# When thirteen stores of zeros are issued: a two-layer decode kernel, forward and backward, on one Trainium2 core

## The chip, the core and the metric

The kernel runs on one core of one Trainium2 chip. A core has a matrix engine (TensorE, PE in the profile; PEld is its weight load), a vector engine (VectorE, DVE), a scalar engine (ScalarE, ACT), a general engine (GpSimd, POOL) and SyncE (SP), which here only issues DMA transfers. All transfers run on 16 DMA engines. SyncE, ScalarE and GpSimd can each issue them: those of SyncE and ScalarE appear in the profile as "hardware_dynamic", those of GpSimd as "software_dynamic". The metric is the time of one launch in device microseconds. Four runs of the kernel before gave 444.23 to 446.92 us, median 445.85.

## What is computed

The reference is the gradient of four residual layers on a single token of width 1024: attention A, MLP B, attention A, MLP B, with the same weights both times. It returns the output, and the gradients of the input, of both caches and of all weights.

```python
def A(x, k_cache, v_cache, wq, wo):      # 32 heads of 128, 4 groups
    W = 4096                             # of 32768 positions, the last ones
    q = x @ wq                           # 1024 x 4096
    p = softmax(q @ k[last W].T * 128**-0.5)
    return (p @ v[last W]) @ wo          # 4096 x 1024
def B(x, w1, b1, w2):                    # 1024 x 3584, 3584 x 1024
    h = x @ w1 + b1
    return (h * tanh(softplus(h))) @ w2
x = x + A(layernorm(x)); x = x + B(layernorm(x))
x = x + A(layernorm(x)); x = x + B(layernorm(x))
out, vjp = jax.vjp(...)                  # returns (out, *vjp(grad_out))
```

Attention looks only at the last 4096 of 32768 cache positions. The gradient of both caches is therefore zero on the other 28672 positions, and these zeros have to be written: 58.7 MB, over half of what the kernel writes (98.84 MB). They depend on nothing, so the kernel may write them at any time.

## The kernel before

Everything is bf16 in memory. The order of the instructions on each engine is the order of the program text; each engine works through its own list, and waits only for what an instruction reads, writes or needs as a buffer. The stages, in order, with their place in the profiled execution (us):

- A1 forward, from 0: K, wq, V and part of wo are loaded and stay.
- B2 forward, from about 59: w1 streams in as 16 half-rows, w2 as 14 chunks of 512 KB through six buffers (`strm`, tag "st"), which all later streams share.
- A3 forward, from about 107.
- B4, 140 to 184 (`mlp_turn`, L711): forward and backward in one. It runs over seven blocks `b` of 512 columns of w1. A block loads two halves (L708), forms h in PSUM, takes mish and its derivative on ACT and DVE (`mish_exp` at L570 first writes y = min(h, 20), L576, then its exponential; `mish_y` at L587 later overwrites y), writes dh and a, and multiplies the transposed block by dh. Between blocks, PE transposes kept weights (`fill`).
- A3 backward, to about 236 (`attn_bwd`, L814).
- The second pass over w2 (`W2Pass.rest`, L646), to about 266: for each of 14 chunks c, PE multiplies and transposes, and DVE forms a row product with a reduction, which yields column c of `wg`.
- The w1 backward (`mlp_bwd_w1`, L795, with `w1_T`, L785), to about 294: 16 steps over half-rows of w1. T(i) loads half-row i and transposes it with PE; ACT and DVE copy the result back over the tile; M(i) multiplies it by dh. The order is M(0), T(2), M(1), T(3) and so on; T(0) and T(1) are put into the end of the w2 pass (hooks "w1", "w1b"). Six buffers hold the tiles, so the load of half-row i can start when M(i - 6) is done.
- A1 backward, to about 329.
- The dW stage, to the end: a list of jobs (L1052, L1285 to L1291) makes the weight gradients of w2, w1, dV, wo, dK, wq as outer products. PE writes PSUM, ACT and DVE evacuate it into 32 buffers, SyncE stores them. `weave` mixes the jobs of two gradients; a few preparing steps (`late_prep`) are inserted at fixed places of the list.

The zeros are cut into 112 stores of 512 KB (L122 to L126), all from one zeroed tile `zt`. Two helpers issue them. `zeros(n)` (L128) lets SyncE issue n of them at its place in SyncE's list. `bg_zeros(n, after)` (L134) lets GpSimd issue n: first a copy of one column of the tile `after`, whose only purpose is that GpSimd waits until that tile is written (a gate), then the stores. Nothing waits for a store of zeros but the end of the kernel, and GpSimd or SyncE themselves, when too many of their transfers are outstanding.

How many are issued where stands in the table `Z` (L1155): `B4` for the seven blocks; `B4w` for chunks of the second w2 pass; `W1` for the start of the w1 backward, behind dh; `W1m`, the steps i at which one store is issued, its gate being the tile of step i - 1; `A1c` in the A1 backward, on GpSimd; `A1d`, later there, on SyncE, where 100 means all that are left. In the kernel before, GpSimd issues 82 stores and SyncE 30.

Of the kernel before, what the change touches and what calls it, by code (L numbers as in the profile page):

```python
# [23 lines left out]
def kernel(  # L24
# [40 lines left out]
    NW2 = TF // 2  # L65
# [11 lines left out]
    def pair_col(kind, lname, n):  # L77

        if kind not in pairs:
            pairs[kind] = keep.tile([P, 2, n], BF16, name=f"{kind}_pair")  # L80
        return pairs[kind][:, 0 if lname in ("A3", "B4") else 1, :]
# [46 lines left out]
    def zeros(n):  # L128
        for _ in range(min(n, len(zero_jobs))):
            nc.sync.dma_start(zero_jobs.pop(0), zt[:])  # L130
# [3 lines left out]
    def bg_zeros(n, after):  # L134

        if n:
            nc.gpsimd.tensor_copy(gate_t[:], after[:, 0:1])
        for _ in range(min(n, len(zero_jobs))):
            nc.gpsimd.dma_start(zero_jobs.pop(0), zt[:])  # L139
# [47 lines left out]
    def xpose(blocks, dst, how=None, six=False):  # L187

        n = len(blocks)
        pools["turn"] += 1  # L190
        if six and pools["turn"] % 6 > 3:
            ps = shaped(pools["top"].tile([P, 1024], BF16, name="tps", tag="h"), [P, 8, P])
        else:
            ps = psum1([P, 8, P], BF16, "tps")
        for b, ap in enumerate(blocks):
            nc.tensor.transpose(ps[:, b, :], ap, ident_bf[:])  # L196
        evac(dst, ps[:, 0:n, :].rearrange("p b c -> p (b c)"), 0.08 * n + 0.05, 0.11 * n + 0.15, how)
# [21 lines left out]
    def wide(n):  # L219
        return Wide(pacc.tile([P, 512], FP32, name="acc", tag="acc"), n)  # L220

    def mv(acc, k, lhsT, vec, start, stop):
        mm(acc.col(k), lhsT, vec.to_broadcast([P, R16]), start, stop)
# [49 lines left out]
    def fill(n, keys, how=None, six=False):  # L273
        for i in range(n):
            for k in keys:
                if xq[k]:
                    ap = xq[k].pop(0)
                    xpose(*nat_blocks(ap), None if how is None else how[i % len(how)], six)
                    break

    def level():
        ev[:] = [0.0, 0.0]

    def ln_fwd(x_col, name):
        xx = work.tile([P, 2 * TD], FP32, name="xx")
        nc.vector.tensor_copy(xx[:, 0:TD], x_col[:])
        nc.vector.tensor_mul(xx[:, TD:], x_col[:], x_col[:])
        sps = sm_tile(P, 2 * TD)
        nc.tensor.matmul(sps[:], lhsT=onesD, rhs=xx[:], start=True, stop=True)
        if name == "A3":  # L290
            warm(6)
        s12 = work.tile([P, 2], FP32, name="s12")
        nc.vector.reduce_sum(s12[:], sps[:].rearrange("p (a b) -> p a b", a=2), axis=AX.X)
        var = work.tile([P, 1], FP32, name="var")
        nc.vector.scalar_tensor_tensor(out=var[:], in0=s12[:, 0:1], scalar=s12[:, 0:1], in1=s12[:, 1:2],
                                       op0=ALU.mult, op1=ALU.subtract, reverse1=True)
        lnv = work.tile([P, 1], FP32, name="lnv")
        nc.scalar.activation(lnv[:], var[:], ACT.Ln, bias=eps_t[:, 0:1], scale=1.0)
        rstd = keep.tile([P, 1], FP32, name=f"rstd_{name}")
        nc.scalar.activation(rstd[:], lnv[:], ACT.Exp, scale=-0.5)  # L300
        n_bf = pair_col("n" + name[0], name, TD)
        nc.vector.tensor_scalar(out=n_bf, in0=x_col[:], scalar1=s12[:, 0:1], scalar2=rstd[:, 0:1], op0=ALU.subtract, op1=ALU.mult)
        n32 = keep.tile([P, TD], FP32, name=f"n32_{name}")
        nc.vector.tensor_scalar(out=n32[:], in0=x_col[:], scalar1=s12[:, 0:1], scalar2=rstd[:, 0:1], op0=ALU.subtract, op1=ALU.mult)
        return n32, n_bf, rstd
# [44 lines left out]
    def wo_load(c):  # L350
        if c < NR:
            w = wo_kept[c]
        else:
            w = strm.tile([P, 2, D], BF16, name="wo_c", tag="st")[:]
        nc.sync.dma_start(w, wo_v[c])
        return w
# [83 lines left out]
    def attn_fwd(x_col, lname, first):  # L440
# [30 lines left out]
        if not first:  # L471
            for c in range(NR, min(NO, NR + NB)):
                held[c] = wo_load(c)
            bg_zeros(Z["A3"], n_bf)
            for w in wq_t:
# [94 lines left out]
    def mish_exp(h_ps, n):  # L570

        def wt(nm):
            return work.tile([P, HQ], FP32, name=nm, tag=nm)[:, 0:n]

        m = {k: wt(k) for k in ("u", "s_", "w_", "r", "hr", "y")}
        nc.vector.tensor_scalar(out=m["y"], in0=h_ps, scalar1=20.0, scalar2=None, op0=ALU.min)  # L576
        nc.scalar.activation(m["u"], m["y"], ACT.Exp)
        return m
# [90 lines left out]
    def mlp_fwd(x_col, lname, g_bf):  # L669
# [5 lines left out]
        for i in range(2 * TD):  # L675
            t, hf = i // 2, i % 2
            w = w1_load(i)
            if i == 0:
                bg_zeros(Z["B2a"], x_col)
            if i == 4:  # L680
# [17 lines left out]
        sv["dact"] = dact  # L698
        x_new, wg = w2.rest(0, g_bf, x_col, f"x_{lname}", gbc, Z["B2"], last)
        return x_new, sv, wg  # L700
# [10 lines left out]
    def mlp_turn(x_col, lname, wg, g_col, nxt):  # L711

        n32, n_bf, rstd = ln_fwd(x_col, lname)
        fill(6, ["V"], "av")
        level()
        sv = dict(n32=n32, rstd=rstd)
        a_bf = pair_col("a", lname, TF)
        dh = keep.tile([P, TF], FP32, name=f"dh_{lname}")
        dh_bf = pair_col("dh", lname, TF)
        sv["dh"], sv["dh_bf"], sv["a_bf"] = dh, dh_bf, a_bf  # L720
        wgf = wg[:].rearrange("p c t -> p (c t)")
        nacc = wide(TD)
        ws = {}
        FB = CB // P

        def M(b):
            w, lo = ws.pop(b), b * FB
            for t in range(TD):
                for f in range(FB):
                    o = (t % HT) * CB + f * P  # L730
                    mv(nacc, t, w[t // HT][:].rearrange("p t f -> p (t f)")[:, o:o + P], dh_bf[:, lo + f:lo + f + 1],
                       b == 0 and t == 0 and f == 0, b == NBK - 1 and f == FB - 1)

        def lo0(b):
            return max(b - 1, 0) * FB

        def X(b, hh):
            wf = ws[b][hh][:].rearrange("p t f -> p (t f)")
            for k in range(2):
                xpose(*alt_blocks(wf[:, k * 1024:(k + 1) * 1024], 4), None, True)  # L740

        for b in range(NBK):
            bg_zeros(Z["B4"][b], dh_bf[:, lo0(b):] if b else n_bf)
            ws[b] = [w1_block(b, hh) for hh in range(2)]
            lo = b * FB
            sl = slice(lo, lo + FB)
            hps = Wide(pacc.tile([P, FB * R16], FP32, name="sm", tag="sm"), FB)
            h_init(hps.t, lo, FB)
            for t in range(TD):
                for f in range(FB):  # L750
                    o = (f // 2) * 2 * P + f % 2
                    mv(hps, f, ws[b][t // HT][:, t % HT, o:o + 2 * P - 1:2], n_bf[:, t:t + 1], False, t == TD - 1)
            m = mish_exp(hps.cols(0, FB), FB)
            X(b, 0)
            mish_w(m, hps.cols(0, FB))
            q = work.tile([P, HQ], FP32, name="q_", tag="hr2")[:, 0:FB]
            nc.vector.tensor_mul(q, wgf[:, sl], m["r"])
            mish_y(m)
            nc.vector.tensor_mul(dh_bf[:, sl], m["y"], q)
            nc.vector.tensor_mul(dh[:, sl], m["y"], q)  # L760
            nc.vector.tensor_mul(a_bf[:, sl], m["hr"], m["w_"])
            ev[0] += 2.4
            ev[1] += 0.3
            if b:
                M(b - 1)
            X(b, 1)
            fill(4, ["wo", "V", "K", "wq"], None, True)
        M(NBK - 1)
        fill(2, ["wo", "V", "K", "wq"], "a")
        g_new, g_bf = ln_bwd(nacc.cols(0, TD), n32, rstd, g_col, lname, nxt)  # L770
        fill(100, ["wo"], "av")
        fill(4, ["V", "K", "wq"], "av")
        level()
        return g_new, g_bf, sv
# [10 lines left out]
    def w1_T():  # L785
# [3 lines left out]
        ws[i] = w  # L789
        if i in Z["W1m"]:  # L790
            bg_zeros(1, ws[i - 1])
# [3 lines left out]
    def mlp_bwd_w1(g_col, lname, sv, nxt):  # L795
# [13 lines left out]
        level()  # L809
        bg_zeros(Z["W1"], sv["dh_bf"])  # L810
        pipe(list(range(2 * TD)), T, M)
# [240 lines left out]
    jobs = []  # L1052

    def run(n):
        for _ in range(min(n, len(jobs))):
            jobs.pop(0)()
# [95 lines left out]
        for _ in range(min(n, len(prep))):  # L1152
            prep.pop(0)()

    Z = dict(B2a=1, B2={0: 1, 4: 1, NW2 - 2: 3}, A3=14, B4=[0, 2, 2, 2, 2, 2, 5], A3c=6, A3d=28, B4w={1: 1, 4: 1, 7: 1, 10: 1}, W1=2, W1m=(3, 6, 9, 12), A1c=3, A1d=100)  # L1155


    x1 = None
# [129 lines left out]
    weave(stage["q"], stage["k"], 2)  # L1288
    for at, f in zip((8, 11, 24, 27, 30, 40, 43, 46, 49, 51, 53), late_prep):
        jobs.insert(at, f)  # L1290
    run(1000)  # L1291
    zeros(1000)
    assert not zero_jobs
# [30 lines left out]
```

## Time and profile before

| what | value |
|---|---|
| median of 4 runs | 445.85 us |
| profiled execution | 446.37 us |
| its span | 444.6 us |
| mean granted TensorE clock | 0.742 |
| PE busy | 321.8 us, 72% |
| DVE busy | 241.3 us, 54% |
| ACT busy | 219.5 us, 49% |
| POOL busy | 62.7 us, 14% |
| moved by DMA | 171.18 MB, mean 385 GB/s |
| read, written in HBM | 71.58 MB, 98.84 MB |
| zero stores on POOL | 82, 10.0 us from issue to landing |
| zero stores on SyncE | 30, 10.4 us from issue to landing |

The span is the time between the first and the last instruction of the execution; 1.8 us lie around it. Busy time is an average over stages with different limits, so the table doesn't say what bounds the kernel. The page's second part cuts the span into 40 slices of 11.1 us and gives each engine's busy share in tenths, the granted clock and what DMA moved; a view by windows gives the same for any stretch. A line of the timeline or of the chain has the start in us, the duration in us, and what ran; square brackets give how long the engine had been idle before, and what ended the wait. A name such as `w_c<-in_B_w_dram` reads: tile w_c, written from the input w1 or w2. SPq is SyncE's queue: its durations are those of issuing transfers, waits between them included, and not of the transfers.

### The profile page before, as it was taken

The page shows a single profiled execution, that of the slowest core. Times are in us where ns is not written, and L with a number is a line of the kernel's source. Part 1 is how long each engine was busy: PE and PEld are TensorE (multiplying, and loading weights), DVE is VectorE, ACT ScalarE, POOL GpSimd, SP SyncE. Part 2 cuts the span into 40 slices and gives each one's busy share as a digit, 9 for nine tenths or more (in the row PEclk, how much of TensorE's full clock was granted, in tenths as well). Part 3 has the DMA queues.
Part 4 walks back from the last instruction along what each step waited for, and adds up shares of the span by engine and source line. Part 5 has one row for each costly group of instructions (what it writes and reads, how often), then busy time and mean ns, then how long its engine had stood idle before and what let it go on. Part 6 is the DMA issues. An engine that isn't in the chain of part 4 may idle for free.

```text
span 444.6 us, 11705 instructions
## 1 busy us (share of the span) xinstructions
PE 321.8 (72%) x5004; PEld 218.0 (49%) x5004; DVE 241.3 (54%) x494; ACT 219.5 (49%) x254; POOL 62.7 (14%) x163
## 2 busy tenths in 40 slices
PE   1565855587979989878897585878967588678830
PEld 0343424477467989766676575856421132211100
DVE  2134101286333766584357554465359889899940
ACT  1122100074153876766865242436037888798940
POOL 2000000011420221152332102114010010000000
PEclk9989555585787998998999559798975555555555
DMA  7999999999999699999999999999999998899997
GB/s 316 424 422 414 407 409 395 407 369 363 412 413 355 213 351 329 384 404 414 415 411 386 388 364 322 367 389 413 417 418 416 419 407 356 353 403 407 419 421 313
DMA packets 48720, 171.18 MB, mean 385 GB/s; under 512 B 4928, under 2 KB 12124, under 8 KB 44572
## 3 DMA queue, kind: packets, MB, share of 16 engines
q1 hardware_dynamic: 36640, 127.16, 73.2%
q0 software_dynamic: 11984, 43.27, 24.5%
q8 instruction: 39, 0.64, 0.5%
q14 instruction: 13, 0.11, 0.1%
q10 hardware_dynamic: 44, 0.01, 0.0%
HBM read 71.58 MB, written 98.84 MB: 383 GB/s over the span
## 4 chain that ended last, share of the span: by engine, by line
PE 23%; DMA 12%; ACT 11%; DVE 4%; issue 2%; POOL 1%; ACTq 0%; SPq 0%; DVEq 0%
DMA w_c<-in_B_w_dram 8%; PE tps L196 6%; PE ops L232 5%; PE acc L232 4%; ACT wq_b L149 3%; ACT K L149 3%; DMA out_dram<-wq_b 2%; ACT st_o L149 2%; DMA out_dram<-st_o 2%; PE sm L232 2%; PE rw L992 2%; ACT V L149 1%; ACT wo_b L149 1%; PE tps L629 1%; PE d L232 1%
## 5 line engine op out<-in xcount | busy, mean ns | idle before, releaser
L232 PEld LDWEIGHTS <-w_c 128*128 128x128 bf16 x1120 | 37.5, 102 | 27.0 <-DMA w_c<-in_B_w_dram 21.0
L139 POOL DMA_DIRECT2D out_dram<-zt x82 | 43.9, 538 | 42.0 <-DMA out_dram<-zt 36.4
L639 ACT COPY w_c<-tps 128x1024 bf16<-128x1024 bf16 x28 | 28.3, 1012 | 30.8 <-PE tps L629 23.5
L653 DVE CUSTOM_DVE_ANT_0 scr<-w_c,gbc 128x1024 bf16<-128x1024 bf16 x28 | 34.2, 1221 | 12.5 <-DMA w_c<-in_B_w_dram 11.2
L232 PE MATMUL ops<-V 2*128 2x512 bf16 (+1 forms) x160 | 33.2, 602 | 4.9 <-ACT V L149 1.2
L149 ACT CAST wq_b<-ops 128x1024 bf16<-128x1024 f32 (+1 forms) x33 | 35.8, 1127 | 1.9 <-PE ops L232 1.8
L146 DVE CAST wq_b<-ops 128x1024 bf16<-128x1024 f32 (+1 forms) x31 | 34.4, 1139 | 2.1 <-PE ops L232 1.6
L149 ACT COPY K<-tps 128x1024 bf16<-128x1024 bf16 x20 | 19.5, 1023 | 29.1 <-PE tps L196 29.0
L232 PEld LDWEIGHTS <-V 128*128 128x128 bf16 (+2 forms) x448 | 16.7, 102 | 33.6 <-issue 32.0
L232 PE MATMUL ops<-wo_b 2*128 2x512 bf16 x120 | 24.0, 569 | 9.8 <-ACT wq_b L149 2.8
L232 PE MATMUL acc<-a_pair,w_c 128*128 128x16 bf16 x448 | 15.8, 172 | 11.3 <-DMA w_c<-in_B_w_dram 11.2
L629 PE MATMUL tps<-ident_bf,w_c 128*128 128x128 bf16 x224 | 23.4, 269 | 0.7 <-DMA w_c<-in_B_w_dram 0.7
L149 ACT COPY w_b<-tps 128x1024 bf16<-128x1024 bf16 x20 | 19.5, 1015 | 6.4 <-PE tps L196 6.3
L196 PE MATMUL tps<-ident_bf,w_c 128*128 128x128 bf16 x224 | 17.3, 237 | 5.8 <-DMA w_c<-in_B_w_dram 5.8
L232 PE MATMUL q<-wq_b,nA_pair 128*32 128x512 bf16 x128 | 11.0, 467 | 14.6 <-DMA wq_b<-in_A_wq_dram 14.3
L146 DVE COPY w_c<-tps 128x1024 bf16<-128x1024 bf16 (+1 forms) x20 | 12.7, 650 | 16.3 <-PE tps L196 11.5
L248 DVE COPY yr<-acc 128x512 f32<-128x512 f32 x6 | 4.2, 692 | 31.4 <-PE acc L232 31.4
L146 DVE COPY K<-tps 128x1024 bf16<-128x1024 bf16 x12 | 8.1, 689 | 23.6 <-PE tps L196 23.6
L232 PEld LDWEIGHTS <-wo_b 2*128 2x128 bf16 (+1 forms) x184 | 7.5, 99 | 27.2 <-issue 24.9
L196 PE MATMUL tps<-ident_bf,K 128*128 128x128 bf16 x256 | 20.4, 242 | 0.0
L149 ACT CAST K<-ops 128x1024 bf16<-128x1024 f32 x17 | 17.1, 1013 | 6.5 <-PE ops L232 6.2
L146 DVE CAST K<-ops 128x1024 bf16<-128x1024 f32 x15 | 18.3, 1222 | 3.1 <-PE ops L232 2.7
(325 smaller groups left out, 662.5 us busy)
## 6 DMA issues: line engine op xcount, KB each, us to landing
out_dram<-zt POOLq DMA_DIRECT2D x82, 512.0 KB, 10.0
out_dram<-zt SPq DMA_DIRECT2D x30, 512.0 KB, 10.4
w_c<-in_B_w_dram SPq DMA_DIRECT2D x32, 448.0 KB, 6.4
w_c<-in_B_w_dram SPq DMA_DIRECT2D x28, 512.0 KB, 7.8
wo_c<-in_A_wo_dram SPq DMA_DIRECT2D x24, 512.0 KB, 7.5
wq_b<-in_A_wq_dram SPq DMA_DIRECT2D x8, 1024.0 KB, 20.7
out_dram<-K SPq DMA_DIRECT2D x8, 1024.0 KB, 9.5
out_dram<-wq_b SPq DMA_DIRECT2D x8, 1024.0 KB, 8.9
```

The source lines that it names most:

```text
L139: nc.gpsimd.dma_start(zero_jobs.pop(0), zt[:])
L146: nc.vector.tensor_copy(out_ap, in_ap)
L149: nc.scalar.copy(out_ap, in_ap)
L196: nc.tensor.transpose(ps[:, b, :], ap, ident_bf[:])
L232: nc.tensor.matmul(out_ap, lhsT=lhsT, rhs=rhs, start=start, stop=stop, skip_group_check=True, **kw)
L248: nc.vector.tensor_copy(yr[:], bank[:])
L629: nc.tensor.transpose(self.ps[c][:, b, :], w[:, 1, b * P:(b + 1) * P], ident_bf[:])
L639: nc.scalar.copy(self.w[c][:, 1, :], self.ps.pop(c)[:].rearrange("p b c -> p (b c)"))
L653: nc.vector.tensor_tensor_reduce(out=scr[:], in0=w[:, 0, :], in1=gbc[:], scale=1.0, scalar=0.0, op0=ALU.mult, op1=ALU.add, accum_out=self. ...
L992: nc.tensor.transpose(ps[:, j, :], sp[:, j, :], ident_bf[:])
```

## The change

Thirteen of the 112 stores get another place, and the number of stores stays. In B4, block 0, two stores are issued behind y instead of none. In the second w2 pass, two are added at its chunk 12, the last but one. In the w1 backward, the two behind dh go, and five single stores at steps 2, 5, 8, 11 and 13 stand where four stood at 3, 6, 9 and 12. In the A1 backward, SyncE issues 23 instead of the 30 left; the last four are issued by SyncE in the dW stage, as two new entries of the job list at places 27 and 33. In SyncE's order these come behind the 7th and behind the 9th of the fourteen stores L1096 from wq_b, the gradient of w1. GpSimd now issues 85 and SyncE 27. The instructions of PE, DVE and ACT keep their number and order.

```diff
@@ mlp_turn
         for b in range(NBK):
-            bg_zeros(Z["B4"][b], dh_bf[:, lo0(b):] if b else n_bf)
+            if b:
+                bg_zeros(Z["B4"][b], dh_bf[:, lo0(b):])
             ws[b] = [w1_block(b, hh) for hh in range(2)]
...
             m = mish_exp(hps.cols(0, FB), FB)
+            if not b:
+                bg_zeros(Z["B4"][b], m["y"])
             X(b, 0)
@@ table
-    Z = dict(B2a=1, B2={0: 1, 4: 1, NW2 - 2: 3}, A3=14, B4=[0, 2, 2, 2, 2, 2, 5], A3c=6, A3d=28, B4w={1: 1, 4: 1, 7: 1, 10: 1}, W1=2, W1m=(3, 6, 9, 12), A1c=3, A1d=100)
+    Z = dict(B2a=1, B2={0: 1, 4: 1, NW2 - 2: 3}, A3=14, B4=[2, 2, 2, 2, 2, 2, 5], A3c=6, A3d=28, B4w={1: 1, 4: 1, 7: 1, 10: 1, 12: 2}, W1=0, W1m=(2, 5, 8, 11, 13), A1c=3, A1d=23)
@@ job list
     for at, f in zip((8, 11, 24, 27, 30, 40, 43, 46, 49, 51, 53), late_prep):
         jobs.insert(at, f)
+    for at in (27, 33):
+        jobs.insert(at, lambda: zeros(2))
     run(1000)
     zeros(1000)
```

## The prediction

> **What bounds the kernel now.** I read, in this order: the slices of the span, busy time by stage, the chain that ended last, and the SyncE queue of the dW stage. First the slices:
>
> ```profile
> DMA  7999999999999699999999999999999998899997
> GB/s 316 424 422 414 407 409 395 407 369 363 412 413 355 213 351 329 384 404 414 415 411 386 388 364 322 367 389 413 417 418 416 419 407 356 353 403 407 419 421 313
> ```
>
> The 16 DMA engines are busy nearly throughout: 171.18 MB at about 415 GB/s would take 412 us of the 444.6 us span. So a store of zeros (512 KB, 0.524 MB, 1.25 us at 420 GB/s) costs time wherever it stands, unless it stands in a hole. The holes are slices 13 to 15, 23 to 25 and 33 to 34. Cut to their edges (columns: busy us of PE, PEld, DVE, ACT, POOL, then clock, DMA share, GB/s):
>
> ```profile
> 145.00:150.00 5.00, 5.00 (x119) 5.00 (x116) 4.36 (x18) 4.07 (x6) 1.25 (x3) 1.00 0.22 76
> 264.00:272.00 8.00, 6.44 (x139) 6.27 (x137) 4.52 (x11) 2.61 (x3) 1.97 (x5) 0.88 0.84 246
> 272.00:284.00 12.00, 7.32 (x141) 7.13 (x138) 3.65 (x7) 3.41 (x4) 1.14 (x4) 0.72 1.02 405
> 284.00:286.00 2.00, 2.00 (x55) 2.00 (x53) 1.21 (x2) 1.52 (x2) 0.30 (x1) 1.00 0.89 218
> 334.00:375.00 41.00, 30.55 (x188) 8.36 (x183) 36.25 (x43) 34.40 (x33) 1.90 (x10) 0.50 1.02 413
> 375.00:381.00 6.00, 4.88 (x38) 1.70 (x31) 6.00 (x11) 4.60 (x5) 0.00 (x0) 0.50 0.52 210
> 381.00:441.00 60.00, 35.86 (x199) 8.55 (x194) 42.66 (x42) 41.27 (x44) 1.02 (x2) 0.50 1.01 413
> ```
>
> The reader is to see three different situations. In 145 to 150 (first block of B4) DMA rests while PE is busy all the time. In 264 to 272 (turn from w2 pass to w1 backward) DMA runs at 246 GB/s, and right after it, 272 to 284, it is full while PE is busy only 7.3 of 12 us: the traffic comes just too late for PE. In 375 to 381 DMA is half idle while DVE is busy 6.00 of 6.00 us. Now the chain of waits in the w1 backward, and TensorE's own row there:
>
> ```profile
> 271.29 9.92 DMA w_c<-in_B_w_dram
> ...
> 285.61 5.70 DMA w_c<-in_B_w_dram
> ```
> ```profile
> 274.04 0.50 PE L232 MATMUL acc<-dh_pair,w_c 128*128 128x16 bf16 x14
> 278.92 1.67 PE L196 MATMUL tps<-ident_bf,w_c 128*128 128x128 bf16 x14 [4.38 <-DMA w_c<-in_B_w_dram]
> ```
>
> PE stands 4.38 us for a w1 load, then runs the transposes at half clock (1.67 us where a step at full clock has 0.94). All its waits for w1 loads come to 5.8 us. And SyncE in the dW stage:
>
> ```profile
> 294.10 40.25 SPq L130 DMA_DIRECT2D out_dram<-zt  x30
> ...
> 357.25 20.93 SPq L1096 DMA_DIRECT2D out_dram<-wq_b  x14
> 379.97 3.08 SPq L1118 DMA_DIRECT2D out_dram<-K  x4
> ```
>
> The thirty zero stores are issued from 294.1 to 334.3, and DMA works the backlog off until the stores of results overtake the engines that make them: from 375 on it waits for evacuations. The K stores of the first dkv go out at 379.97, the moment DVE ends the last evacuation (378.69 + 1.22 = 379.91). From 381 to 441 DMA is full: the 4.2 + 8.4 + 8.4 + 4.2 MB of K, wo, wq, K take 60 us. **So the end is: start of the dW stage (329.8) + about 50 us of engine time to the K stores + 60 us of DMA + 3.6 us.** Backlog before 375 isn't in that sum.
>
> **The change, part by part.** It moves thirteen stores; their number stays 112, POOL's share goes from 82 to 85.
>
> *Two stores in B4.* The gate reads y, written at 145.41 + 0.16 = 145.57 by L576. POOL idles (13.02 us before its next gate at 148.10), so gate 145.6, issue 146.1 to 147.2. The next pair was issued at 148.57 and DMA was full from 150: 1.2 us later. So the new pair moves 2.5 us of data from 147.3 to 149.8, just ahead of the old pair. Nothing of DMA's later work shifts; cost 0, cover the hole of 5 us. The DVE write that must wait for the gate's read of y (L590, 147.42) is 1.6 us behind it. If the cover fails, one thing is exposed: PE waited 1.6 and 1.7 us ("issue", at 165.84 and 185.25) with DMA full; an instruction fetch (queue q8) lies at 148.2 by the packet records and would now meet traffic. Bounds 0 to 1.7 us; I take 0.2, since most such fetches in full DMA (a dozen between 90 and 190) made no wait.
>
> A rule speaks against every store put on POOL: the Trainium skill, SBUF — State Buffer, section "SBUF: two separate sides", says that VectorE in a two-port mode locks GpSimd out so that it can't write the descriptors; its example of a 620 ns DMA took 3100. The row: the 82 zero issues took 533 ns in the median and 715 at most, among them those at 268.9 and 283.76 between DVE's copies. By the rule each POOL store would come 2.5 us late; the pair of c = 12 below would then flow where the old pair flowed, and the -2.9 below would be about 0. By the row nothing is late. I take the row.
>
> *w2 pass and w1 backward.* Removed: the pair behind dh_pair (issued 268.90, 269.43) and the four at steps 3, 6, 9, 12. Added: a pair when wg of c = 12 is there (DVE's read at 262.08, so issue 262.6 to 263.7), and singles at steps 2, 5, 8, 11, 13. Each single's gate is the transposed tile of the step before; going by the DVE copies and the old gates (270.24 for step 3), the first two are issued at about 267.8 and 272.9, the others one step ahead of the old ones. What this does to DMA: in 264 to 272 it moved 246 x 8 = 1.97 MB; at 415 it could have moved 3.32, so 1.35 MB fit. PE ends step M(5) at 274.5, having waited for no load from 264 on, so loads have slack here: by the packet records loads 2 to 5 had been moved by 269.3, and T(5) runs at 272.12. The pair and the single of step 2, 1.57 MB, land in this trough; 0.2 MB spill over.
> After 272, up to the last load (asked for at 285.61, there at 291.3), DMA carried in the old order five stores (the pair, steps 3, 6, 9) and now three (steps 5, 8, 11; the single of step 13, like the old one of step 12, is issued too late to come before the last load). So 2 x 0.524 - 0.2 = 0.85 MB less: 2.0 us at 420 GB/s. On top of that, the low stretch 284 to 286 (218 GB/s, (420 - 218) x 2 = 0.4 MB, 1.0 us) exists because PE's late M steps freed no buffers for loads 12 to 15; without the long wait I take 0.9 us of it as won. Sum **-2.9 us**. Ends: from 0 (all of it spent on loads 3 to 5) to -7.3 (PE's 5.8 us of waits and two half-clock transposes at 0.73 each gone), which DMA's own limit forbids; with the dip untouched -2.0, with the spill at nothing -3.4.
>
> A second rule bears on the slack: DMA: Bandwidth & Descriptors, section "Queues, rings and completion order": each engine goes round-robin between its queue rows by packets. By it the pair halves the pace of loads 3 to 5 while it lasts, and they are done up to 2.5 us late, at 271.8, 0.3 us ahead of T(5). The row nearest is the single store issued at 258.18: by the packet records it moved only from 261.2, behind loads asked for before it; by that, loads 3 and 4 go first. Both leave T(5) unharmed, the rule barely. This is where the rival below starts.
>
> *dW stage.* Thirty stores become 23, with four more behind the 7th and the 9th of the stores of w1's gradient from wq_b. The backlog ends 7 x 1.25 = 8.75 us earlier, near 335; the first chunk is evacuated by then (331.1), so DMA goes on. From there its demand is 14 x 1.25 + 9 x 1.1 = 27 us for the first 23 chunks, done near 363.6 though the next chunk is evacuated at 363.2: about there the hole now begins, and there the four stores (5 us) go. Three stores less up to the K stores means 3.75 us more idle DMA, not an earlier K store: that waits for DVE and ACT. Cost 0, gain 0; cover: some 6 us of idle DMA between 365 and 381. Without this cover it would be +1.25 us a store.
>
> A1's own stage keeps its three POOL stores and its PE chain, in which no wait for DMA stands (its longest is 1.7 us, for POOL). So what the w1 backward gains passes through to the dW start, and to the end. **Sum: +0.2 - 2.9 + 0 = -2.7 us** on the profiled execution of 446.37 (span 444.6 and 1.8 around it): 443.7. This execution lies 0.5 above the median 445.85, so the forecast for the median is **443.2**, a gain of 0.6%. A change within 0.5% (2.2 us: 443.6 to 448.1) can't be told from none here.
>
> **The rivals.**
> *A, the trough fills but the gain is eaten (445.4, -0.5).* Before the last load there are now six stores where there were five: +1.25 us; and the single of step 13 delays the first wo loads of A1. For it: loads dominate the chain here. Against: A1's six products over wo on DVE (L837) run without a wait for DMA. Chance 0.20.
> *B, slower: the pair overtakes the loads (448.6, +2.7).* If stores at c = 12 and step 2 delay load 5 past 272.1, PE waits there instead of at 274.5, its M steps free buffers late, and the trough only moves. Then one store more costs 1.25 us, and two more transposes run at half clock (0.73 each): +2.7. It decides from the point where load 5 is over 2.8 us later than now (272.1 - 269.3). Chance 0.14.
> *C, the end hangs on DMA alone (439.5).* If backlog counts after all, the three stores taken out of the tail are worth 3.75 us besides the 2.7. For it: the last 60 us are DMA. Against: the hole at 375 to 381. Chance 0.12.
> The forecast's own mechanism has 0.54.
>
> **How the numbers follow.** The forecast's own range is -1.2 to -4 us (441.9 to 444.6); of its 0.54 I put 0.38 below 443.6 and 0.16 above. Faster: 0.38 + 0.12 = 0.50. Same: 0.16 + A's 0.20 + 0.02 of B = 0.38. Slower: the rest of B, 0.12. The range 440.8 to 447.6 takes in the forecast, A and the near edge of B and C, and leaves out some 0.19.
>
> **What would show it.** Right: DMA share near 1 in 147 to 150 and over 350 GB/s in 264 to 272; PE's 4.38 us wait below 1.5; the A1 stage starting 2 to 4 us earlier; in the dW stage holes near 365 and before the K stores, these still leaving as DVE ends. Wrong: a PE wait for w_c before 273; the last w1 load no earlier than 290; K stores that leave later than 50.2 us behind the first evacuation; a tail from K to the end that isn't 60 us.

## The result, and the profile after

The change gave 444.54 us (median of 35 runs) where the kernel before gave 445.96 (56 runs). The ratio is 0.9987, with a 95% interval of 0.9968 to 1.0007: a gain of 0.6 us, between 1.4 faster and 0.3 slower. The forecast was 443.2, a gain of 2.7 us. So the time lies inside the range, which was wide, and by the ratio the gain can't be told from none. The ratios here leave out every run that lies more than 1.5% above the fastest of its kernel, which drops between none and half of a kernel's runs, so the tables below also give the difference of the means of all runs, with its 95% half-width. That difference is -1.0 ± 0.9 us for the change. Medians are of all runs, and single runs of one kernel have a standard deviation of about 2 us.

The profiled execution took 444.55 us, with a span of 442.8. Its slices, DMA share and rate:

```profile
DMA  7999999999999999999999999999999986999997
GB/s 316 423 423 413 406 408 390 407 369 372 412 412 351 363 338 346 396 380 410 416 411 389 363 397 409 405 416 416 417 368 405 404 320 274 368 402 406 419 423 303
```

Slice 14 (213 GB/s before) has 363, slice 25 (322 before) has 409. The hole that is left is in slices 33 to 35, in the dW stage. Both holes that were to be filled are filled in this execution. The windows of the change, in the columns of the prediction (busy us of PE, PEld, DVE, ACT, POOL, then clock, DMA share, GB/s):

```profile
145.00:150.00 5.00, 5.00 (x130) 5.00 (x127) 4.09 (x18) 4.25 (x6) 1.25 (x3) 1.00 1.04 398
264.00:272.00 8.00, 6.37 (x123) 6.11 (x121) 4.45 (x11) 1.99 (x3) 0.72 (x2) 0.79 1.02 411
272.00:284.00 12.00, 9.74 (x224) 9.27 (x222) 5.86 (x9) 6.22 (x8) 2.35 (x7) 1.00 1.02 402
284.00:286.00 2.00, 1.74 (x39) 1.74 (x40) 0.69 (x1) 0.70 (x1) 0.78 (x2) 1.00 1.02 412
365.00:381.00 16.00, 12.97 (x89) 4.07 (x81) 15.30 (x21) 13.76 (x14) 0.00 (x0) 0.50 0.70 283
```

The first block of B4 now moves 398 GB/s (76 before), the turn 264 to 272 moves 411 (246 before), in 272 to 284 PE is busy 9.74 of 12 us (7.32 before), and the low stretch 284 to 286 has 412 GB/s (218 before). TensorE's own row at the w1 backward has its first wait for a w1 load at T(6), of 0.71 us; the 4.38 us are gone. The half-clock transposes are not gone but stand earlier: T(3), before that wait, takes 1.65 us, and from 272 on the clock is full:

```profile
268.52 1.65 PE L196 MATMUL tps<-ident_bf,w_c 128*128 128x128 bf16 x14
...
273.89 0.96 PE L196 MATMUL tps<-ident_bf,w_c 128*128 128x128 bf16 x14 [0.71 <-DMA w_c<-in_B_w_dram]
```

SyncE's queue in the dW stage, in the same form as before:

```profile
289.73 31.41 SPq L130 DMA_DIRECT2D out_dram<-zt  x23
...
348.88 8.39 SPq L1099 DMA_DIRECT2D out_dram<-wq_b  x7
357.32 2.84 SPq L130 DMA_DIRECT2D out_dram<-zt  x2
361.25 2.80 SPq L1099 DMA_DIRECT2D out_dram<-wq_b  x2
364.10 1.11 SPq L130 DMA_DIRECT2D out_dram<-zt  x2
365.74 10.43 SPq L1099 DMA_DIRECT2D out_dram<-wq_b  x5
377.98 3.08 SPq L1121 DMA_DIRECT2D out_dram<-K  x4
```

For an account of the two executions I cut the kernel at points that every trace has: the layer norm ahead of B4 (L286), dh ahead of the w1 backward, the layer norms at the end of the w1 backward and of the A1 backward (L310), the first evacuation of the dW stage, and the first K store. I call **the stretch** what lies from B4 to the end of the w1 backward. The windows of the change: stretch, w1 backward, A1 backward, dW stage up to the K store:

```profile
138.15:289.31 151.16, 127.39 (x2557) 114.06 (x2557) 88.46 (x230) 90.66 (x106) 36.99 (x83) 0.90 1.01 386
266.36:289.31 22.95, 19.30 (x420) 18.47 (x420) 10.57 (x17) 10.02 (x12) 3.37 (x10) 0.93 1.03 408
289.31:324.38 35.07, 30.17 (x400) 19.00 (x400) 16.17 (x39) 9.79 (x13) 7.30 (x27) 0.85 1.03 416
327.78:377.98 50.20, 37.28 (x225) 10.22 (x221) 45.39 (x56) 42.38 (x41) 2.99 (x19) 0.50 0.86 344
```

And of the kernel before, the same four:

```profile
139.69:293.68 153.99, 126.61 (x2557) 115.78 (x2557) 88.71 (x231) 90.93 (x106) 35.16 (x78) 0.88 0.98 365
268.12:293.68 25.56, 18.98 (x420) 18.43 (x420) 10.53 (x18) 10.02 (x12) 4.37 (x12) 0.87 0.95 345
293.68:326.38 32.70, 27.79 (x400) 17.41 (x400) 16.18 (x39) 9.76 (x13) 7.30 (x27) 0.95 1.03 417
329.78:379.97 50.19, 37.27 (x225) 10.20 (x221) 45.39 (x56) 42.38 (x41) 3.16 (x19) 0.50 0.98 394
```

Between the two executions: -1.54 us ahead of B4 (138.15 against 139.69), where nothing was changed; -2.83 in the stretch; +2.37 in the A1 backward; +0.01 up to the K stores; +0.17 behind them. Sum -1.82, the difference of the two spans. Three things in it need an experiment: the first and the third number sit where no instruction was moved, and the stretch gained as much as forecast, while the whole kernel did not. One pair of profiles can't tell the effect of two stores from the scatter. So the parts were run alone.

### The profile page after: what moved, and what is told of

It reads as the page before. It is cut to its first block, busy times and chain, and to the rows that moved or that the text cites. A ratio compares the mean times of both kernels' runs of the same rounds, so it can differ in the third digit from the quotient of the medians.

```text
span 442.8 us, 11711 instructions
## 1 busy us (share of the span) xinstructions
PE 324.0 (73%) x5004; PEld 218.0 (49%) x5004; DVE 241.1 (54%) x494; ACT 219.5 (50%) x254; POOL 64.3 (15%) x168
## 4 chain that ended last, share of the span: by engine, by line
PE 25%; ACT 12%; DMA 9%; DVE 4%; issue 2%; POOL 1%; ACTq 0%; DVEq 0%; SPq 0%
PE tps L196 7%; DMA w_c<-in_B_w_dram 6%; PE ops L232 6%; PE acc L232 5%; ACT wq_b L149 3%; ACT K L149 3%; DMA out_dram<-wq_b 2%; ACT st_o L149 2%; PE sm L232 2%; ACT V L149 2%; PE rw L995 2%; ACT wo_b L149 1%; PE d L232 1%; PE tps L629 1%; PE wps L155 1%
## 5 line engine op out<-in xcount | busy, mean ns | idle before, releaser
L139 POOL DMA_DIRECT2D out_dram<-zt x85 | 45.4, 537 | 41.6 <-DMA out_dram<-zt 35.4
L629 PE MATMUL tps<-ident_bf,w_c 128*128 128x128 bf16 x224 | 23.7, 271 | 0.8 <-DMA w_c<-in_B_w_dram 0.8
L232 PE MATMUL q<-wq_b,nA_pair 128*32 128x512 bf16 x128 | 9.8, 424 | 15.9 <-DMA wq_b<-in_A_wq_dram 15.9
L196 PEld LDWEIGHTS <-K 128*128 128x128 bf16 x256 | 16.9, 107 | 5.1 <-issue 5.0
```

Source lines behind the costliest of these rows:

```text
L232: nc.tensor.matmul(out_ap, lhsT=lhsT, rhs=rhs, start=start, stop=stop, skip_group_check=True, **kw)
L629: nc.tensor.transpose(self.ps[c][:, b, :], w[:, 1, b * P:(b + 1) * P], ident_bf[:])
```

## The experiments

The kernels ran in five jobs, each on one chip, with the kernel before in every job. In the tables, "us" is the ratio minus one, times the median of the kernel before in the same job (445.8 to 446.9 us); "us, all runs" is the difference of the means.

### The parts one by one

e1 has only the part in the second w2 pass and the w1 backward, e2 only the pair in B4, e3 only the four stores in the dW stage, e4 all but the pair in B4. Against the kernel before:

```diff
# e1
-    Z = dict(... B4w={1: 1, 4: 1, 7: 1, 10: 1}, W1=2, W1m=(3, 6, 9, 12), ...)
+    Z = dict(... B4w={1: 1, 4: 1, 7: 1, 10: 1, 12: 2}, W1=0, W1m=(2, 5, 8, 11, 13), ...)
# e2
-    Z = dict(... B4=[0, 2, 2, 2, 2, 2, 5], ...)     # and the gate on m["y"]
+    Z = dict(... B4=[2, 2, 2, 2, 2, 2, 5], ...)
# e3
-    Z = dict(... A1d=100)
+    Z = dict(... A1d=26)
+    for at in (27, 33):
+        jobs.insert(at, lambda: zeros(2))
# e4: e1 and e3 together, A1d=25
```

> Only the w2/w1 part of the change (pair at chunk 12, none behind dh, singles at steps 2, 5, 8, 11, 13); B4 and the dW stage as before, SyncE stores the 29 left in the A1 backward. Theory 1, the B4 stores cost PE its instruction fetch: this kernel has the gain without that cost, time 443.2 (-2.7 us, ratio 0.994), with dh to the A1 backward's layer norm near 23.0 us (25.6 before). Theory 2, the A1 backward gives the gain back through a lower granted clock: ratio 0.9985 to 1.000, layer norm to layer norm in A1 near 35 us (32.7 before). Theory 3, the gain in the w1 backward is real only because B4's stores were taken out of its way: dh to layer norm stays at 25 us, ratio 1.000.

> Only the two stores behind y in block 0 of B4; SyncE stores the 28 left in the A1 backward. Theory 1: PE's waits put down to issue in B4 rise from 3.3 to 5 us or more, B4 takes 1 to 2.5 us longer, ratio 1.002 to 1.006. Theory 2: no effect before A1, ratio 1.000. Theory 3: with two stores less behind it nothing changes before A1 either, 1.000.

> Only the dW part: SyncE stores 26 in the A1 backward and 2 + 2 at places 27 and 33 of the job list. All three theories: first evacuation to the K stores 50.2 us, K stores to the end 64.6 us, as in both profiles; ratio 1.000 (0.998 to 1.002). If the tail hung on DMA alone or the four stores delayed the K stores, it would differ by up to 5 us.

> The change without its B4 part (the w2/w1 and dW parts; SyncE stores 25 and 4). Theory 1: faster than the change, ratio to before 0.993 to 0.995. Theory 2: like the change, 0.9985. Theory 3: like before, 1.000.

| kernel | median us (runs) | ratio to before | 95% interval | us | us, all runs |
|---|---|---|---|---|---|
| e1, w2 pass and w1 backward | 443.71 (22) | 0.9936 | 0.9902 to 0.9970 | -2.9 | -2.5 ± 1.0 |
| e2, B4 pair | 445.01 (14) | 1.0003 | 0.9972 to 1.0034 | +0.1 | -0.7 ± 1.2 |
| e3, dW stores | 445.52 (22) | 1.0023 | 0.9995 to 1.0051 | +1.0 | -0.3 ± 0.9 |
| e4, without the B4 pair | 444.10 (22) | 0.9952 | 0.9922 to 0.9983 | -2.1 | -2.4 ± 1.2 |

The part in the w1 backward alone has the forecast gain. Each other part has an interval that holds zero. The change without the pair is faster than before, with an interval that ends below 1; that of the change itself reaches beyond 1. That points at the pair, but the two intervals overlap (up to 0.9983, from 0.9968), and e2, which has only the pair, shows no cost by either measure.

The view that matters for the pair is the first block of B4 in kernels that issue nothing there, the same five microseconds counted from the layer norm. First e1, then f2 (below), then f4 (below), then e4, where the kernel before had 76 GB/s:

```profile
142.40:147.40 5.00, 5.00 (x122) 5.00 (x120) 4.06 (x17) 4.66 (x6) 1.24 (x3) 1.00 0.82 281
```
```profile
143.40:148.40 5.00, 5.00 (x124) 5.00 (x122) 4.07 (x17) 4.76 (x6) 1.24 (x3) 1.00 0.68 237
```
```profile
140.80:145.80 5.00, 4.89 (x115) 4.90 (x116) 3.79 (x16) 3.59 (x5) 1.24 (x3) 1.00 0.96 309
```
```profile
144.00:149.00 5.00, 5.00 (x121) 5.00 (x118) 4.37 (x18) 4.05 (x6) 1.24 (x3) 1.00 0.43 146
```

**The hole on which the forecast let the pair lie was a draw.** By the packet records, DMA's idle time in the first 15 us of B4 was 4.1 us in the profile of before, but 0.7 to 4.7 us, in the mean 2.5, over eleven profiles of kernels without the pair (before included; g4 below isn't counted). Over seven with the pair it was 0.2 to 2.3, in the mean 1.5. So the pair fills about 1.0 us of idle DMA in the mean, while its 1.05 MB need 2.7 us at the stretch's 386 GB/s. By this estimate the other 1.7 us are traffic that pushes later traffic; that is worked out from means that scatter by 1 us, and not measured on its own.

### Is it the pair, and does the tail give anything back?

f1 is the change once more, f2 is e4 once more. f3 issues four stores there instead of two, taking two more from SyncE's. f4 is the kernel before without the last eight of SyncE's zero stores: 4 MB of one cache gradient's zeros are not written.

```diff
# f3, against the change
-    Z = dict(... B4=[2, 2, 2, 2, 2, 2, 5], ... A1d=23)
+    Z = dict(... B4=[4, 2, 2, 2, 2, 2, 5], ... A1d=21)
# f4, against before
-    Z = dict(... A1d=100)
+    Z = dict(... A1d=22)
-    zeros(1000)
+    del zero_jobs[:]
```

> The change once more, beside its own version without the B4 part on the same chip. Theory B (the two stores of B4 cost what the w1 backward gains, since the hole they were meant for isn't there in every execution): ratio to before 0.997 to 1.001, slower than the version without them by 1.2 to 2 us. Theory N (the first measurement of the change and that of its parts differ by chance, B4's stores are free): both 0.994 to 0.996, within 0.6 us of each other. In both: dh to the layer norm of the A1 backward near 23 us; in A1 the time follows the half-clock stretch, 32.0 us with none, 32.7 with 3.4, 33.3 with 6.8, 35.1 with 10.2 us of it.

> The change without its B4 part, once more. Theory B: ratio to before 0.993 to 0.996, and 1.2 to 2 us faster than the whole change. Theory N: 0.994 to 0.996, equal to the whole change.

> The change with four stores behind y in B4 instead of two, two less by SyncE in the A1 backward (21). Theory B: two more stores in front of a stretch that DMA bounds, 1.25 us each where no hole is left: 1.5 to 2.5 us slower than the change, ratio to before 1.001 to 1.006. Theory N: the hole of 5 us (DMA at 76 GB/s in 145 to 150 of before) holds four stores: equal to the change.

> The kernel before with 22 of the 30 stores of SyncE in the A1 backward; the last eight are left out, so 8 x 512 KB of one cache gradient aren't written. If the end is the start of the dW stage + 114.9 us whatever the backlog (my sum), the ratio is 1.000 (0.997 to 1.003), first evacuation to end 114.9, DMA idle for some 10 us more before the K stores. If the tail hangs on DMA alone, it is 8 x 1.25 = 10 us faster, ratio 0.978.

| kernel | median us (runs) | ratio | 95% interval | us | us, all runs |
|---|---|---|---|---|---|
| f1, the change | 444.41 (14) | 0.9981 | 0.9951 to 1.0012 | -0.8 | -1.5 ± 1.0 |
| f2, without the pair | 444.56 (22) | 0.9947 | 0.9919 to 0.9976 | -2.4 | -1.8 ± 1.0 |
| f3, four in B4 | 447.13 (22) | 1.0031 | 1.0010 to 1.0053 | +1.4 | +1.3 ± 1.1 |
| f4, eight left out in the tail | 446.59 (22) | 1.0025 | 1.0002 to 1.0048 | +1.1 | +0.6 ± 0.9 |

f3 settles that stores in this block are not free: with four of them the whole gain of the other parts is lost, and 1.4 us more. From two (f1) to four is 2.2 us by the ratios and 2.9 ± 1.2 over all runs. From none (mean of e4 and f2: 0.9949) to four (1.0031) is 3.7 us, 0.9 a store.

What the first pair costs is not resolved. The change ran in three jobs (0.9987, 0.9981 and, in a later one, 0.9952; weighted 0.9975), which puts the pair at 1.2 us; with the widths of the intervals combined, at 0 to 2.3. The medians (444.1 and 444.56 without, 444.41 to 444.54 with) don't show it. Over all runs the same five measurements put it at 0.7 ± 1.0, f1 and f2 of one job at 0.3 ± 1.2, and e2 puts it at -0.7 ± 1.2. The profiles don't decide either: with the new places in the w1 backward the stretch is 152.3 us in the mean of five with the pair (151.2 to 154.2) and 150.7 in three without (148.0 to 153.8), but with the old places it is 152.6 with it (e2) and 153.5 to 155.1 without (before, e3, f4, h3). Of f3 only the times are used here.

f4 settles the other end of the kernel. Eight stores left out altogether did not make it faster. The dW stage of f4, from the first evacuation to the K store:

```profile
325.74:375.94 50.20, 37.28 (x226) 10.22 (x221) 45.38 (x56) 42.37 (x41) 3.13 (x19) 0.50 0.77 309
```

Again 50.20 us, with DMA at 0.77 where it had 0.98. Rival C, by which the backlog counts, expected 0.978. From the first evacuation to the end f4 takes 114.85 us, before 114.81. That f4 is 1.1 us slower by the ratio has no place in its profile, and over all runs the difference holds zero.

### Stores taken out where DMA bounds

If the price of a store is set by the stretch, it must also come back when stores leave it. g1 is e1 with two stores fewer in the A3 backward (GpSimd issues 26 instead of 28; SyncE issues the two in A1), g4 the same with six fewer. g3 takes two from the A3 backward of the kernel before. g2 is e1 without the single store of step 13, the last one ahead of A1.

```diff
# g1, against e1; g3 the same against before; g4 with A3d=22
-    Z = dict(... A3d=28, ...)
+    Z = dict(... A3d=26, ...)
# g2, against e1
-    Z = dict(... W1m=(2, 5, 8, 11, 13), ...)
+    Z = dict(... W1m=(2, 5, 8, 11), ...)
```

> The w2/w1 part of the change alone, and 26 instead of 28 stores of GpSimd in the A3 backward (SyncE stores 31 in the A1 backward). Theory D (from B4 to the A1 layer norm DMA bounds, 385 GB/s, so each store of 0.524 MB taken out of that stretch into the tail is worth 1.36 us until the tail's idle DMA ahead of the K stores, 2 to 3 us, is used up): 2.7 us faster than the w2/w1 part alone (0.9936), 440.5 us, ratio 0.988 (0.985 to 0.991). Theory P (PE's own chain bounds the stretch, B4's pair cost through PE's waits there): like the w2/w1 part alone, 0.993 to 0.996.

> The w2/w1 part without its fifth single (step 13): pair at chunk 12, singles at steps 2, 5, 8, 11; so as many stores in the stretch as before, SyncE stores 30. Theory D: one store less than in the w2/w1 part, 0.5 to 1.3 us faster than it (the single of step 13 comes late in the stretch), ratio 0.990 to 0.9925. Theory P: the same as the w2/w1 part, 0.993 to 0.996.

> The kernel before with 26 instead of 28 stores of GpSimd in the A3 backward, SyncE stores 32. Theory D: 2.7 us off the stretch, of which the tail gives back at most 0.4 (2.5 us more backlog, 2.2 of idle DMA): ratio 0.994 to 0.996. Theory P: 1.000.

> The w2/w1 part alone with 22 stores of GpSimd in the A3 backward; SyncE stores 35. Theory D: six stores out of the stretch, -8.2 us, but the tail has room for some 3 us only, so the K stores are followed by DMA work that starts 4.5 us late: net -3.7 against the w2/w1 part alone, ratio 0.985 to 0.988, the first evacuation to the end 119.5 instead of 114.9. Theory P: nothing won in the stretch and 4.5 lost in the tail, ratio 1.003.

| kernel | median us (runs) | ratio | 95% interval | us | us, all runs |
|---|---|---|---|---|---|
| g1, w1 part, two out of A3 | 442.49 (22) | 0.9913 | 0.9885 to 0.9941 | -3.9 | -3.8 ± 1.1 |
| g2, w1 part, no store at 13 | 442.80 (22) | 0.9917 | 0.9890 to 0.9944 | -3.7 | -2.7 ± 1.3 |
| g3, before, two out of A3 | 443.31 (22) | 0.9942 | 0.9917 to 0.9967 | -2.6 | -2.5 ± 1.0 |
| g4, w1 part, six out of A3 | 443.37 (22) | 0.9909 | 0.9881 to 0.9936 | -4.1 | -2.9 ± 1.3 |

g3 is the cleanest of all: one number of the kernel before is changed, two stores go from the A3 backward to SyncE's list in A1, and it wins 2.6 us (1.5 to 3.7), 1.3 a store (0.524 MB at 386 GB/s is 1.36). Its stretch and its dW stage up to the K store, from an execution that was the shortest of its 22, so that the stretch's 5.7 us against before are not all the stores' doing:

```profile
139.78:288.10 148.32, 126.75 (x2557) 115.26 (x2557) 88.11 (x231) 90.56 (x106) 34.00 (x76) 0.88 0.99 376
323.57:373.77 50.20, 37.27 (x225) 10.19 (x221) 45.38 (x56) 42.38 (x41) 2.97 (x19) 0.50 1.02 410
```

The dW stage has 410 GB/s (before 394), and its idle DMA, 2.2 us before, is used up to less than 0.1; the 50.20 us stay. The two stores are free there. g1 (expected 0.985 to 0.991) came out just above its band. Against e1 it wins 1.0 us, only 0.5 a store, in another job. g4 missed its band of 0.985 to 0.988: six stores bring no more than two. Its traced execution was its longest (449.62 us) and so only hints at where the return ends. DMA is full up to the first K store, the K stores come 0.3 us later than in all other profiles, and the end follows 66.9 us behind the first of them, where most kernels have 64.4 to 64.9:

```profile
330.41:380.91 50.50, 37.58 (x228) 10.46 (x223) 45.70 (x56) 42.67 (x41) 3.09 (x19) 0.50 1.02 409
```

Where between two and six the return ends was not looked for. g2 lies within 0.8 us of e1; what the store of step 13 costs is not resolved.

### Is the A1 backward's longer time the change's doing?

h1 is the change with two stores fewer in the A3 backward. h2 and h3 are the change and the kernel before with eight instead of five filler products of PE (`warm`) in the layer norm that starts A1. k2 is the change and k3 is h2, side by side. k1 is g1 with the longer filler.

```diff
# h2, h3, k3, k1 (ln_bwd)
         if nxt == "A1":
-            warm(5)
+            warm(8)
# h1, against the change; k1: A3d=26 as in g1
-    Z = dict(... A3d=28, ...)
+    Z = dict(... A3d=26, ...)
```

> The whole change, with 26 instead of 28 stores of GpSimd in the A3 backward (SyncE stores 25 in the A1 backward and the 4 in the dW stage). If B4's pair costs only because its bytes stand in the stretch that DMA bounds, two stores out of the same stretch give its cost back: ratio 0.992 to 0.9955, the stretch from B4 to the A1 layer norm 2 to 3 us shorter than the change's 151.3, the tail 114.9 us. If B4's pair costs through its place (PE's waits there, GpSimd's gate), taking stores out of A3 doesn't give it back: 0.997 to 1.000.

> The whole change, with eight instead of five idle matmuls on PE in the layer norm backward ahead of A1; nothing else. If the lower granted clock in A1 (both profiles of the change: 35.1 us, mean clock 0.85) is brought on by the change and by PE's rest there, A1 falls to 32 to 33 us and the ratio to 0.992 to 0.995. If the clock's phase is chance, the ratio stays at 0.9985 (0.996 to 1.001).

> The kernel before with the same eight matmuls. By either view 1.000 (0.997 to 1.003), A1 at 32 to 33.3 us; if before too loses time there in many executions, up to 0.5% faster.

> The version that the runs so far point to: the w2/w1 part alone, 26 stores of GpSimd in the A3 backward, eight idle matmuls ahead of A1. If bytes in the stretch and the clock in A1 are two separate losses: 0.987 to 0.9905. If eight matmuls only help where B4's pair stands: 0.990 to 0.993, as without them (0.9913).

> The whole change, on the same chip as its version with eight matmuls. By its two measurements so far 0.9985 (0.996 to 1.001). If A1's lower clock belongs to the change, A1 takes 35 us again.

> The whole change with eight idle matmuls ahead of A1, once more. If the first measurement (0.9945) was the clock in A1 and no chance, 0.9935 to 0.996, 1.2 to 2.4 us faster than the change beside it, A1 at 32 us. If it was chance, within 0.7 us of the change.

| kernel | median us (runs) | ratio | 95% interval | us, all runs | A1 backward us |
|---|---|---|---|---|---|
| h1, change, two out of A3 | 444.19 (12) | 0.9964 | 0.9934 to 0.9993 | -2.4 ± 1.2 | 32.90 |
| h2, change, longer filler | 443.92 (12) | 0.9945 | 0.9912 to 0.9977 | -2.5 ± 1.6 | 31.96 |
| h3, before, longer filler | 446.15 (12) | 0.9991 | 0.9954 to 1.0028 | +0.1 ± 1.8 | 31.86 |
| k1, g1, longer filler | 440.42 (6) | 0.9849 | 0.9810 to 0.9888 | -6.7 ± 1.1 | 31.94 |
| k2, change | 444.42 (22) | 0.9952 | 0.9927 to 0.9977 | -1.8 ± 1.0 | 31.96 |
| k3, change, longer filler | 444.56 (22) | 0.9967 | 0.9941 to 0.9994 | -2.0 ± 1.0 | 32.94 |

The A1 backward follows how long TensorE ran at half clock in it: 0, 3.4, 6.8 or 10.2 us of half clock go with 31.9 to 32.0, 32.6 to 33.1, 33.3 and 35.1 us. The change drew 10.2 in two profiles and none in the third (k2); g1, without the pair, drew 10.2 too; e1 drew none. So **the +2.37 us of the two profiles are within chance**, as far as one to three profiles of a kernel can tell. So are the -1.54 us ahead of B4: all kernels here are the same up to there, and their profiles take 135.5 to 142.6 us for it. Side by side the filler wins nothing (k3 against k2); h2's gain was not repeated.

h1 missed its expectation, which says that SyncE would store 25 in A1. That was a slip: `A1d=23` still holds, so the two stores were left over and issued behind the last K store, at the end of everything. Its SyncE queue:

```profile
423.02 4.22 SPq L1121 DMA_DIRECT2D out_dram<-K  x4
427.29 2.56 SPq L130 DMA_DIRECT2D out_dram<-zt  x2
```

The slip measures something. h1's stretch is 147.8 us, 3.3 shorter than the change's; its tail, from the first evacuation to the end, is 117.4 where every other profile but g4's has 114.6 to 115.1. Two stores cost their transfer time again where DMA runs to the end with nothing behind it: 2.4 us. So h1's time doesn't tell whether two stores out of the A3 backward give back what the pair costs, which it was built to tell.

**The faster version.** k1 is the fastest of all: 440.42 us, ratio 0.9849, in six runs; g1, without the filler, has 0.9913 in 22. Since the filler won nothing in the other pair, I take k1's surplus over g1 for unexplained. Both beat the change and the kernel before. In short: take the w1 part, leave the pair out of B4, and take two stores out of the A3 backward.

## Why the prediction was wrong in its sum, and right in its largest part

**The w2 pass and w1 backward: -2.9 forecast, -2.9 measured in e1 (-4.4 to -1.3).** That the two agree to the digit is luck, with an interval of 3 us and -2.5 over all runs; the way and the size are right. The trough filled, PE's long wait went, and load 5 came in time: the first wait for a load is that of T(6), at 273.89, where T(5) had been the one in danger. The section's own length agrees: from dh to the layer norm it took 25.6 to 28.2 us, mean 26.5, in the six profiles with the old places, and 22.9 to 25.9, mean 23.7, in the twelve with the new ones, 2.8 less. Part of that may only have left the section, since the pair now goes out ahead of dh. The whole stretch, which the move doesn't leave, is 153.5 to 155.1 us, mean 154.1, with the old places and no pair in B4, and 150.7 in the mean of e1, e4 and f2, 3.4 less with the scatter given above. Rival B, by which the pair overtakes load 5, is out. So is the POOL rule as a price here: the 85 issues took 533 ns in the median and 715 at most, and the stores landed after 9.8 us in the median (10.0 before). Rival A's size (445.4) is about what was measured, but its mechanism is not seen: e1, which has both of the places that it named, has the whole gain.

**The dW stage: 0 forecast.** The frame of "about 50 us of engine time to the K stores" held to 0.03 us in every profile read, with 7.3 us of idle DMA in it (the change), 11.8 (f4) and less than 0.1 (g3); only g4, which fills it, has 50.50. Rival C is refuted by f4. e3's +1.0 us has an interval that holds zero, turns into -0.3 ± 0.9 over all runs, and has no place in its profile (114.82 us from the first evacuation to the end, before 114.81). The prediction's sum for the end is 1 us short, because it lets the 60 us start at 381 and not at the K stores (379.97): from these to the end it is 64.6 us. That cancels in a difference.

**A1 passes the gain through:** right in the mean, as far as the profiles tell; in a single one its half-clock time hides or doubles the gain.

**The step that failed is the B4 pair: "Nothing of DMA's later work shifts; cost 0, cover the hole of 5 us", taken at +0.2.** Two assumptions in it fell, though how much the first pair itself costs stays open. The hole was read from one execution, and that one was among the emptiest: 4.1 us idle where the mean is 2.5. And what the hole doesn't hold isn't free, for DMA is the bound from there to the end of the w1 backward (share 1.01 over the 151 us of the change): g3 shows 1.3 us for each of two stores in that stretch, f3 0.9 for each of four in this very block. The first pair costs 1.2 us by the ratios of the kernels with and without it (0 to 2.3; e2 alone: -1.2 to 1.5), 0.7 ± 1.0 over all runs, and by the estimate above about 1.7 through what it leaves unfilled. Its 0.2 is thus too low by the first and the last of these, and not excluded by the second. The bound that the prediction gave, 0 to 1.7 us, holds the three values, but not for the reason named there: PE's "issue" waits in B4 and the A3 backward come to 3.3 us before, 5.9 after, 1.0 in f1, 2.3 in e2 and 4.6 in e3, which has no pair, so they don't follow the pair.

The working had said in its second sentence that a store costs time wherever it stands, unless in a hole. It applied that to the tail and to the w1 backward, and for the pair took a hole in one profile for a property of the kernel. With 1.2 in place of 0.2, the sum is -1.7, against -0.6 in the first comparison (-1.4 to +0.3) and -1.1 in the mean of three; over all runs the three give -1.4 ± 0.6. The remaining half microsecond to one can't be assigned with these intervals, and its cause stays open. Nor is everything of one piece: h1, with the pair, has the same stretch as g1 without it (147.8 and 147.9 us), in one profile each.

## What to carry to other kernels

Price a background transfer by what bounds the stage it stands in: bytes divided by the rate where DMA is the bound up to the next stage that engines set, nothing where engines set the pace, up to that stage's idle DMA. So move such transfers from the first kind of stage to the second until its idle time is used up, as g3 did, and not the other way round, as the B4 pair did. A hole in one profile is one draw: look at the same place in several executions, or in several kernels that don't differ there, before it serves as cover in a sum.

## What was not expected of the hardware

- DMA counted as full moved 386 GB/s in the mixed stretch (loads and stores together) and 416 in the A1 backward, both at a share of 1.01 or more. At these rates 512 KB take 1.36 and 1.26 us.
- The dW stage up to the K store repeats to 0.03 us over all the profiles but g4's, while the stretch took 153.8 and 150.3 us in two executions of one kernel (e4 and f2). Within the stretch, B4 and the A3 backward together took either 90.4 to 91.2 or 93.5 to 97.9 us; the shorter one is followed by a w2 pass and w1 backward of 57.1 to 64.6 us, the longer by 53.2 to 59.7. Only the whole stretch can be compared.
- The half clock comes in steps of 3.4 us in the A1 backward (in all profiles but g4's, with 8.0), and their number differs between executions of the same kernel (10.2, 10.2 and 0 for the change).
